# Sketch attention and squared-ReLU FFN: sketch features by TensorE products, block transposes and squares on VectorE, denominators as an extra column of kv

## The chip, the cores and the metric

One core of a Trainium2 chip. The time is device microseconds of one execution; medians of several executions are quoted. A profile's span is one or two microseconds shorter than the time of its run. The engines are TensorE (PE in the profile, PEld for its weight loads), VectorE (DVE), ScalarE (ACT), GpSimd (POOL) and SyncE (SP), which issues most DMAs. A run is called slow when it lies more than 1.5% above the fastest of its kernel.

## The reference, cut to what matters

```
q, k, v: (4 batches, 4 heads, 1088, 32);  S1, S2: (8, 32)      all fp32
phi(x)[i, j] = (S1 x)[i] * (S2 x)[j]            # 64 features of a token and head
kv  = sum over tokens of phi(k) v               # 64 x 32 per head
z   = sum over tokens of phi(k)                 # 64 per head
att = (phi(q) kv) / (phi(q) z + 1e-6)
x   = att as (4352 tokens, 128)
out = relu(x w_in)^2 w_out                      # 128 -> 2048 -> 128
```

## The kernel before: what the change and the argument touch

Tokens are handled in tiles of 128. The sketch products S1 x and S2 x are made by hand: GpSimd permutes q and k, GpSimd and VectorE multiply them with a broadcast row of S1 and S2 (4096 products per token for q and k together), VectorE adds in eights and GpSimd finishes the sums.

```python
for ti in range(2):                       # q, k
    for h in range(H):
        onpool = pcnt < NPOOL_PROD        # 3 of 8 on GpSimd
        pcnt += 1
        eng = nc.gpsimd if onpool else nc.vector
        src1 = ssperm if onpool else ssp_ps
        eng.tensor_tensor(                # L351
            out=_pap(Pa, 0, ns, 2048 * ti + 512 * h, [[1, 512]]),
            in0=_pap(xP, 0, ns, 128 * ti + 32 * h, [[0, 16], [1, 32]]),
            in1=_pap(src1, 0, ns, 0, [[32, 16], [1, 32]]), op=mult)
nc.vector.tensor_reduce(                  # L357
    out=Vt[0:ns, :], in_=_pap(Pa, 0, ns, 0, [[8, 512], [1, 8]]), axis=AX, op=add)
# ... GpSimd: Vt -> Wt -> av (two halvings), then 64 feature products per head
# ... TensorE transposes the features of q and k tile by tile into qkT; ScalarE copies
```

The denominators have a path of their own in each batch's "tail": z by a VectorE sum, broadcast by TensorE, permuted copies and products on GpSimd (`qpP`, `Pd`), and three more VectorE sums (`Vd`, `Wd`, `den`). The FFN runs in chunks of 512, 512 and 64 tokens:

```python
nc.tensor.matmul(pg[:, 0:nt], w_in[:, 128*c : 128*c+128], xT[:, t0 : t0+nt])   # fp16
nc.scalar.activation(gt[:, 0:nt], pg[:, 0:nt], Relu)
nc.scalar.activation(g2[:, 0:nt], gt[:, 0:nt], Square)
nc.tensor.matmul(po[:, 0:nt], w_o[:, 128*c : 128*c+128], g2[:, 0:nt], ...)      # fp32
```

## Time and profile before

| | |
|---|---|
| time, median of 4 runs | 553.76 us (550.21 to 558.77) |
| first FFN product starts | 187.9 us |
| last VectorE-heavy stretch ends | about 490 us |

Page of the kernel before: busy time per engine, then the span in 40 equal slices, where a digit is the busy share in tenths (PEclk: the granted TensorE clock in tenths).

```profile
PE 360.0 (66%) x1562; PEld 217.6 (40%) x1562; DVE 400.7 (73%) x652; ACT 225.6 (41%) x562; POOL 322.5 (59%) x726
...
PE   1021222591445599997455999984439999999996
...
DVE  1899996799999996889999968789997120580000
...
POOL 0999997579954685589846865897553000530000
PEclk9999999999999999995555999955559998559998
```

VectorE stands mostly at 8 or 9 in the first three quarters; TensorE is nearly idle in the first third and busy after. No average tells this: the windows view of the kernel before does, with the busy time of each engine in three stretches (then clock, DMA share, GB/s).

```profile
20.00:183.00 163.00, 57.34 (x276) 42.51 (x276) 153.53 (x189) 18.02 (x35) 135.40 (x302) 1.00 0.14 22
183.00:440.00 257.00, 201.82 (x879) 116.26 (x880) 220.71 (x348) 138.27 (x342) 167.41 (x371) 0.79 0.08 16
440.00:549.00 109.00, 98.78 (x406) 58.30 (x404) 20.97 (x108) 66.08 (x184) 12.35 (x33) 0.82 0.03 9
```

The columns after the length are PE, PEld, DVE, ACT, POOL. The clock of 1.00 in the first line is no measurement: this trace has no clock record before 192.7 us, and the views count such time as full clock. The durations say otherwise (18 instructions of `kv_ps` took 2.20 us at 111.7 us and 1.28 at 225.7). For 163 us VectorE is 94% busy and TensorE 35%; only the last 109 us belong to TensorE. The groups view of the kernel before (line, engine, operation, tiles, count; busy us and mean ns of one; idle before it):

```profile
L357 DVE TENSOR_REDUCE Vt<-Pa 128x512 f32<-128x4096 f32 (+1 forms) x36 | 158.6, 4406 | 0.2
L351 POOL TENSOR_TENSOR Pa<-xP,ssperm 128x512 f32<-128x512 f32 (+1 forms) x108 | 134.7, 1258 | 0.0
L351 DVE TENSOR_TENSOR Pa<-xP,ssp_ps 128x512 f32<-128x512 f32 (+1 forms) x180 | 114.9, 672 | 5.9 <-POOL xP L336 5.9
```

The sketch products and their first sum are 273.5 us of VectorE's 400.7. The chain of waits of the kernel before, by engine:

```profile
PE 40%; DVE 28%; POOL 20%; issue 7%; ACT 5%; DMA 0%; ACTq 0%; SPq 0%; POOLq 0%
```

### The profile page before, as it was taken

To read this page: it belongs to the slowest core of one execution; us is meant where nothing else is said; L and a number is where in the kernel's file an instruction comes from. 1 tells how busy PE (TensorE), PEld (TensorE's weight loads), DVE (VectorE), ACT (ScalarE), POOL (GpSimd) and SP (SyncE) were. 2 spreads that over 40 slices of the span, in tenths; PEclk is the share of its full clock that TensorE was granted. 3 is DMA by queue.
4 is the path that set the end of the run, shared out by engine and by line. 5 is a ranking of instruction groups with operands and counts; after the bars stand their busy time and mean duration, and the time that the engine had idled before them with its cause. 6 is when DMAs were issued, how large, how long until landed. Compare 5 with 4: busy or idle time off the path is not lost.

```text
span 549.1 us, 5863 instructions
## 1 busy us (share of the span) xinstructions
PE 360.0 (66%) x1562; PEld 217.6 (40%) x1562; DVE 400.7 (73%) x652; ACT 225.6 (41%) x562; POOL 322.5 (59%) x726
## 2 busy tenths in 40 slices
PE   1021222591445599997455999984439999999996
PEld 0011111470334244466342444673313346973334
DVE  1899996799999996889999968789997120580000
ACT  2010111011000389672003896720018977118885
POOL 0999997579954685589846865897553000530000
PEclk9999999999999999995555999955559998559998
DMA  5431011012000001022000010000000000000000
GB/s 163 69 61 19 14 20 20 11 24 36 7 10 10 10 11 38 11 38 39 10 10 12 11 39 11 20 16 1 0 2 2 10 11 19 4 0 1 11 9 22
DMA packets 61424, 11.39 MB, mean 21 GB/s; under 512 B 54864, under 2 KB 61264, under 8 KB 61264
## 3 DMA queue, kind: packets, MB, share of 16 engines
q1 hardware_dynamic: 61392, 11.02, 10.4%
q8 instruction: 12, 0.20, 0.1%
q14 instruction: 20, 0.16, 0.1%
HBM read 8.78 MB, written 2.23 MB: 20 GB/s over the span
## 4 chain that ended last, share of the span: by engine, by line
PE 40%; DVE 28%; POOL 20%; issue 7%; ACT 5%; DMA 0%; ACTq 0%; SPq 0%; POOLq 0%
PE po L114 24%; POOL Pa L351 9%; DVE Vt L357 9%; PE pg L105 5%; DVE Pa L351 4%; PE kv_ps L189 3%; DVE Wd L231 3%; DVE xs_big L271 3%; POOL xP L336 3%; DVE den L243 2%; POOL qpP L207 2%; POOL qp_big L387 2%; POOL Wt L370 2%; ACT gt L112 1%; DVE Vd L225 1%
## 5 line engine op out<-in xcount | busy, mean ns | idle before, releaser
L357 DVE TENSOR_REDUCE Vt<-Pa 128x512 f32<-128x4096 f32 (+1 forms) x36 | 158.6, 4406 | 0.2
L351 POOL TENSOR_TENSOR Pa<-xP,ssperm 128x512 f32<-128x512 f32 (+1 forms) x108 | 134.7, 1258 | 0.0
L351 DVE TENSOR_TENSOR Pa<-xP,ssp_ps 128x512 f32<-128x512 f32 (+1 forms) x180 | 114.9, 672 | 5.9 <-POOL xP L336 5.9
L112 ACT ACTIVATE gt<-pg 128x512 f32<-128x512 f32 (+1 forms) x192 | 82.1, 472 | 15.3 <-PE pg L105 15.0
L370 POOL TENSOR_TENSOR Wt<-Vt 128x256 f32<-128x256 f32 (+1 forms) x36 | 21.9, 609 | 72.1 <-DVE Vt L357 45.1
L213 POOL TENSOR_TENSOR Pd<-qpP,Zp_sb 128x256 f32<-128x256 f32 (+1 forms) x36 | 25.8, 727 | 52.5 <-ACT Zp_sb L199 52.5
L105 PE MATMUL pg<-xT,w_in 128*128 128x512 f16 (+1 forms) x192 | 53.1, 334 | 3.2 <-ACT gt L112 2.0
L336 POOL COPY xP<-qt 128x32 f32<-128x32 f32 (+1 forms) x144 | 27.6, 232 | 36.7 <-DVE Pa L351 23.8
L207 POOL COPY qpP<-qp_big 128x64 f32<-128x64 f32 (+1 forms) x144 | 37.9, 309 | 0.4
L177 DVE COPY zr<-zr_ps 1x64 f32<-1x64 f32 x16 | 3.3, 208 | 41.2 <-PE zr_ps L175 41.2
L105 PEld LDWEIGHTS <-w_in 128*128 128x128 f16 x192 | 20.1, 111 | 28.9 <-issue 26.9
L189 PE MATMUL kv_ps<-vt_big,kp_big 128*64 128x32 f32 (+1 forms) x288 | 27.9, 252 | 0.3 <-DVE zr L177 0.3
L336 POOL COPY xP<-kt 128x32 f32<-128x32 f32 (+1 forms) x144 | 27.7, 233 | 0.0
L189 PEld LDWEIGHTS kv_ps<-vt_big,kp_big 128*64 128x64 f32 (+1 forms) x288 | 24.7, 168 | 4.6 <-issue 1.1
L271 DVE TENSOR_SCALAR xs_big<-xs_big,rm 128x128 f32<-128x128 f32 (+1 forms) x36 | 23.7, 660 | 0.0
L231 DVE TENSOR_TENSOR Wd<-Vd 128x8 f32<-128x8 f32 (+1 forms) x36 | 23.7, 670 | 0.0
L387 POOL TENSOR_TENSOR qp_big<-av 128x256 f32<-128x256 f32 (+1 forms) x36 | 22.4, 621 | 0.2
L387 POOL TENSOR_TENSOR kp_big<-av 128x256 f32<-128x256 f32 (+1 forms) x36 | 22.4, 621 | 0.0
L243 DVE TENSOR_SCALAR den<-den 128x4 f32<-128x4 f32 (+1 forms) x36 | 20.7, 576 | 0.0
L196 ACT COPY kv_sb<-kv_ps 64x32 f32<-64x32 f32 x16 | 2.9, 180 | 37.4 <-PE kv_ps L189 37.3
L225 DVE TENSOR_REDUCE Vd<-Pd 128x16 f32<-128x256 f32 (+1 forms) x36 | 14.6, 405 | 3.5 <-POOL Pd L213 3.5
L290 ACT CAST xT<-xt_ps 128x128 f16<-128x128 f32 (+1 forms) x36 | 8.2, 258 | 19.0 <-PE xt_ps L285 19.0
(942 smaller groups left out, 780.9 us busy)
## 6 DMA issues: line engine op xcount, KB each, us to landing
qt<-in_q_dram SPq DMA_DIRECT2D x32, 64.0 KB, 2.0
kt<-in_k_dram SPq DMA_DIRECT2D x32, 64.0 KB, 2.2
vt_big<-in_v_dram SPq DMA_DIRECT2D x32, 64.0 KB, 2.4
out_dram<-ot_sb SPq DMA_DIRECT2D x32, 64.0 KB, 1.6
w_in_95<-in_moe_w_in_dram SPq DMA_DIRECT2D x1, 1024.0 KB, 5.1
w_o<-in_moe_w_out_dram SPq DMA_DIRECT2D x16, 64.0 KB, 2.0
vt_big<-in_v_dram SPq DMA_DIRECT2D x4, 32.0 KB, 2.2
qt<-in_q_dram SPq DMA_DIRECT2D x4, 32.0 KB, 2.1
```

Of the source, the lines that this page charges most:

```text
L105: nc.tensor.matmul(pg[:, 0:nt], w_in[:, 128 * c : 128 * c + 128], xT[:, t0 : t0 + nt],)
L112: nc.scalar.activation(gt[:, 0:nt], pg[:, 0:nt], Relu)
L114: nc.tensor.matmul(po[:, 0:nt], w_o[:, 128 * c : 128 * c + 128], g2[:, 0:nt], start=(g == 0 and cc == 0), stop=(g == 7 and cc == 1),)
L189: nc.tensor.matmul(kv_ps[:, :], _pap(kp_big, 0, ns, st * 256 + 64 * h, [[1, 64]]), _pap(vt_big, 0, ns, st * 128 + 32 * h, [[1, 32]]), star ...
L207: nc.gpsimd.tensor_copy(out=_pap(qpP, 0, ns, 64 * h, [[16, 4], [4, 4], [1, 4]]), in_=_pap(qp_big, 0, ns, st * 256 + 64 * h + 12, [[1, 4], ...
L231: nc.vector.tensor_tensor(out=Wd[0:ns, :], in0=_pap(Vd, 0, ns, 0, [[2, 8]]), in1=_pap(Vd, 0, ns, 1, [[2, 8]]), op=add,)
L271: nc.vector.tensor_scalar(out=_pap(xs_big, 0, ns, st * 128, [[1, 128]]), in0=_pap(xs_big, 0, ns, st * 128, [[1, 128]]), scalar1=rm[0:ns, 0 ...
L336: nc.gpsimd.tensor_copy(out=_pap(xP, 0, ns, 128 * ti + 32 * h, [[8, 4], [4, 2], [1, 4]]), in_=_pap(xt, 0, ns, 32 * h + 12, [[1, 4], [16, 2 ...
L351: eng.tensor_tensor(out=_pap(Pa, 0, ns, 2048 * ti + 512 * h, [[1, 512]]), in0=_pap(xP, 0, ns, 128 * ti + 32 * h, [[0, 16], [1, 32]]), in1= ...
L357: nc.vector.tensor_reduce(out=Vt[0:ns, :], in_=_pap(Pa, 0, ns, 0, [[8, 512], [1, 8]]), axis=AX, op=add,)
L370: nc.gpsimd.tensor_tensor(out=Wt[0:ns, :], in0=_pap(Vt, 0, ns, 0, [[2, 256]]), in1=_pap(Vt, 0, ns, 1, [[2, 256]]), op=add,)
L387: nc.gpsimd.tensor_tensor(out=_pap(pp_big, 0, ns, st * 256, [[64, 4], [8, 8], [1, 8]]), in0=_pap(av, 0, ns, 64 * ti, [[16, 4], [1, 8], [0, ...
```

## The change

Its intent: let TensorE do the sketch products, so that VectorE and GpSimd no longer bound the first part. Three named parts: features by fp32 products on TensorE (q and k transposed in 32x32 blocks by VectorE); the denominators as a 33rd column of kv (a column of ones beside v); squares on VectorE. With them comes a new structure: whole-batch loads of q and k; q features made already transposed, so no features are transposed afterwards; FFN chunks of 384, 384 and 320 tokens; and the attention of batch b+1 spread over the FFN of batch b, one piece for each four FFN steps. Cut to its core:

```diff
-  # permuted copies, products Pa, sums Vt, Wt, av; feature products on GpSimd; transposes
+  nc.vector.transpose(kT[:, c0:c1], kn[:, c0:c1])          # 32x32 blocks; L159, q: L162
+  nc.tensor.matmul(kf[0:w, ...64], kT[:, 128*t : 128*t+w], sk[:, :])        # L170, fp32
+  nc.scalar.copy(fb, second half of kf)
+  nc.vector.tensor_tensor(out=kp, in0=kf broadcast, in1=fb broadcast, op=mult)   # L187
+  nc.tensor.matmul(kvp[:, 66*pr : 66*pr+66], kp 128 columns, va 66 columns, ...) # L197
+  # q: features of two heads at a time, 64 rows of S1 / S2 and of q
+  nc.tensor.matmul(pa[:, 0:n], sqa[64*pr : 64*pr+64, :], qT[64*pr : 64*pr+64, c0:c0+n])  # L217
+  nc.scalar.copy(sa[:, 0:n], pa[:, 0:n])
+  nc.tensor.matmul(pb[:, 0:n], sqb[64*pr : 64*pr+64, :], qT[64*pr : 64*pr+64, c0:c0+n])  # L224
+  nc.vector.tensor_tensor(out=qp[...], in0=pb[:, 0:n], in1=sa[:, 0:n], op=mult)           # L227
-  # z, zp, qpP, Pd, Vd, Wd
+  # column 32 of each head's 33 columns of nd is the denominator
+  nc.tensor.matmul(nd[0:w, o : o+66], qp[... w columns], kv_sb[:, 66*pr : 66*pr+66])      # L241
-  nc.scalar.activation(g2[:, 0:nt], gt[:, 0:nt], Square)
+  nc.vector.tensor_tensor(out=g2[:, 0:n], in0=gt[:, 0:n], in1=gt[:, 0:n], op=mult)        # L321
+  for t0, t1 in CHUNKS:
+      for i, _ in enumerate(ffn_gen(b, t0, t1)):
+          if i % 4 == 2:
+              next(nxt, None)                  # a piece of attn_gen(b + 1)
```

## The prediction

> **What bounds the kernel now.** Page part 1: VectorE 400.7 us busy of 549 (73%), TensorE 360.0, GpSimd 322.5, ScalarE 225.6. Windows view: from 20 to 200 us almost only attention runs (VectorE 82 and 89 us of each 90, TensorE 24 and 49); from 200 to 440 attention of the next batch and FFN overlap, VectorE 85% busy; after 440 FFN remains, bound by TensorE and ScalarE. The chain of waits is PE 40%, DVE 28%, POOL 20%. Sketch features are made by hand (groups view): products (POOL 134.7, DVE 114.9 us) and an eight-wide sum (DVE 158.6 us). The squares cost ScalarE 0.63 us per 512 columns.
>
> **What the change does (estimates, per batch).**
> - TensorE. FFN stays: per 512 columns the trace has 0.213 us for the fp16 product and 0.86 for the fp32 one at full clock, so 0.8 us for 384; 36 us per batch. Added: 45 fp32 products with new 128-column weights and 64 or 66 moving columns. Four such of 32 columns (nd) took 1.08 us at full clock and 1.91 at half, so about 0.30 each: 14 us; four streams of 1088 columns: 7 us; transposes 2. About 59 us, 236 in all.
> - VectorE. Loses products, sums and the denominator's small ops. Gets squares, 48 x 0.48 us = 23; tails 8; feature products 6; block transposes 2.5. The Trainium skill, "VectorE: DVE Perf Modes", section "Mode 1× (REGULAR) — the baseline", gives one result per cycle; the trace agrees (512 elements in 0.672 us). About 40, 160 in all.
> - ScalarE. Relu 48 x 0.47 = 23 us, plus copies: 33; about 135 in all.
> - GpSimd: from 322 to a few us.
> - DMA: whole-batch q and k loads, 16 v loads of 128-byte rows. About 0.5 us of issue each, hidden.
>
> So the bound moves from VectorE plus GpSimd to TensorE, and FFN of batch b runs beside attention of b+1 throughout. The program order puts several first-layer products ahead of the second-layer ones, so I expect few stalls.
>
> **Time.** Opening: loads, transposes, attention of batch 0 with a cold TensorE, first FFN product at about 34 us (before: about 183). Then FFN 145 + attention of three batches 69 + rest of batch 0 6 = 220 us, with 8% for waits: 238. Output tail 4, clock dips 9: **285 us**, range 262 to 325. Chances: faster by over 2% 0.99, within 2% 0.005, slower 0.005.
>
> The clock matters: in the second half of the trace the same work ran at 0.5 whenever TensorE was sparse or fed by short products (250-300, 357-410, 462-492 us). The Trainium skill, "TensorE: Matmul & The Clock Gate", Part 1, says the array runs at half rate when idle; 1.08 against 1.91 us agrees. The denser stream should hold full clock nearly throughout after the opening.
>
> **What would show it right.** TensorE busy over 85% from 40 us on; granted clock near 1.0; VectorE near 160 us, ScalarE near 135, GpSimd under 15; the chain of waits dominated by PE (po, pg); squares about 0.5 us; first FFN product near 34 us.
>
> **What would make it wrong.** (a) Each FFN step now crosses ScalarE and VectorE, in-order queues: a square behind a block of tail ops, or a wait for the single-buffered attention accumulator in TensorE's order, would stall TensorE; then TensorE idles on DVE, and 320 us. (b) Bursts of short fp32 products drop the clock to 0.5 in each batch: 5 to 15 us more per batch. (c) Block transposes or PSUM-read feature products much slower than one element per cycle. (d) A longer opening, if loads come late.

## The result and the profile after

The changed kernel takes 288.06 us (287.52 to 288.63, 4 runs), against 553.76 us. The ratio is 0.5207, 95% interval 0.5188 to 0.5227. Here and below a ratio is the mean time of one kernel's fast runs over that of the other's of the same rounds, so not quite the ratio of the quoted medians. The prediction was 285 us, range 262 to 325.

Page of the kernel after, the same rows as before:

```profile
PE 260.4 (91%) x1104; PEld 157.9 (55%) x1104; DVE 153.9 (54%) x441; ACT 114.2 (40%) x302; POOL 2.2 (1%) x17
...
PE   0578996999999999999989999999899999999991
...
DVE  0810106569634587937346788655345784653550
...
POOL 2000000000000000000000000000000000000000
PEclk9999999999999999999999999999999999999997
```

TensorE is busy from slice 7 to the end, VectorE about half the time, GpSimd not at all. Chain of waits of the kernel after, by engine and by line:

```profile
PE 86%; DVE 4%; ACT 3%; DMA 3%; issue 2%; ACTq 0%; DVEq 0%
PE po L322 43%; PE pg L315 10%; PE pb L224 7%; PE kvp L197 7%; PE nd L241 7%; PE pa L217 6%; PE kf L170 4%; ACT gt L320 2%; DMA kn<-in_k_dram 2%; PE op L337 2%; DVE qp L227 1%; PE xp L300 1%; ACT oT L331 0%; ACT sa L222 0%; DMA s_nat<-in_S_dram 0%
```

Windows view of the kernel after, the columns as before, from the first FFN product on:

```profile
53.30:60.00 6.70, 6.70 (x21) 4.11 (x22) 4.82 (x17) 2.79 (x8) 0.00 (x0) 1.00 0.00 0
60.00:280.28 220.28, 215.29 (x965) 128.37 (x963) 133.63 (x379) 102.02 (x274) 0.16 (x1) 1.00 0.08 21
```

From 60 us to the last FFN product TensorE is 98% busy. So the story of the prediction holds, and the total too. But its first stage does not: the first FFN product came at 53.3 us, not at 34. The timeline of the kernel after shows why. Twelve instructions of `nd`, the second group of batch 0 and then the same group of batch 1:

```profile
50.73 2.77 PE L241 MATMUL nd<-kv,qp 128*128 128x66 f32 x12
...
106.76 1.50 PE L241 MATMUL nd<-kv,qp 128*128 128x66 f32 x12
```

Until about 58 us TensorE runs at half rate, although it is 76 to 100% busy in each 10 us from 10 us on. Note that the PEclk row says 9 up to the last slice. The row counts time before the first clock record as full clock, and the first record of this trace starts at 58.4 us, with full clock; so the row does not show a cold start, and the durations do. The Trainium skill, "TensorE: Matmul & The Clock Gate", section "Seeing it yourself", warns that the recorded clock events can be unreliable; here the record at 58.4 us agrees with the durations, and only the row read from the records is wrong, by a factor of two for the 48 us before it.

So three questions are left. Why was the opening cold for so long? If the opening took 19 us more than predicted, what took 19 us less? And which parts of the change brought the 266 us?

### The profile page after: what moved, and what is told of

The parts are those of the page before. It is cut to its first block, busy times and chain, and to the rows that moved or that the text cites. A ratio compares the mean times of both kernels' runs of the same rounds, so it can differ in the third digit from the quotient of the medians.

```text
span 286.6 us, 3493 instructions
## 1 busy us (share of the span) xinstructions
PE 260.4 (91%) x1104; PEld 157.9 (55%) x1104; DVE 153.9 (54%) x441; ACT 114.2 (40%) x302; POOL 2.2 (1%) x17
## 4 chain that ended last, share of the span: by engine, by line
PE 86%; DVE 4%; ACT 3%; DMA 3%; issue 2%; ACTq 0%; DVEq 0%
PE po L322 43%; PE pg L315 10%; PE pb L224 7%; PE kvp L197 7%; PE nd L241 7%; PE pa L217 6%; PE kf L170 4%; ACT gt L320 2%; DMA kn<-in_k_dram 2%; PE op L337 2%; DVE qp L227 1%; PE xp L300 1%; ACT oT L331 0%; ACT sa L222 0%; DMA s_nat<-in_S_dram 0%
## 5 line engine op out<-in xcount | busy, mean ns | idle before, releaser
L320 ACT ACTIVATE gt<-pg 128x384 f32<-128x384 f32 (+1 forms) x192 | 78.2, 480 | 70.3 <-PE pg L315 68.2
L315 PE MATMUL pg<-xTb,w_in 128*128 128x384 f16 (+1 forms) x192 | 47.4, 323 | 2.6 <-ACT gt L320 2.1
L224 PE MATMUL pb<-qT,sqb 64*128 64x512 f32 (+1 forms) x48 | 25.2, 610 | 3.7 <-DVE qp L227 2.0
L217 PE MATMUL pa<-qT,sqa 64*128 64x512 f32 (+1 forms) x48 | 25.7, 621 | 0.9 <-DVE qp L227 0.9
L197 PEld LDWEIGHTS kvp<-va,kp 128*128 128x128 f32 (+1 forms) x144 | 22.0, 225 | 6.3 <-issue 5.5
L170 PE MATMUL kf<-sk,kT 128*128 128x64 f32 (+1 forms) x72 | 13.8, 334 | 12.4 <-DVE sk L125 10.3
L197 PE MATMUL kvp<-va,kp 128*128 128x66 f32 (+1 forms) x144 | 23.1, 309 | 0.0
L241 PE MATMUL nd<-kv,qp 128*128 128x66 f32 (+1 forms) x144 | 22.1, 294 | 0.0
L241 PEld LDWEIGHTS nd<-kv,qp 128*128 128x128 f32 (+1 forms) x144 | 20.2, 208 | 2.8 <-issue 1.5
L187 DVE TENSOR_TENSOR kp<-kf,fb 128x256 f32<-128x256 f32 (+1 forms) x36 | 13.2, 411 | 6.4 <-PE kvp L197 5.1
```

The lines of the kernel that those rows point to most:

```text
L170: nc.tensor.matmul(kf[0:w, 64 * i : 64 * i + 64], kT[:, 128 * (t0 + i) : 128 * (t0 + i) + w], sk[:, :],)
L187: nc.vector.tensor_tensor(out=_ap(kp, 0, w, 256 * i, [[64, 4], [8, 8], [1, 8]]), in0=_ap(kf, 0, w, 64 * i, [[16, 4], [1, 8], [0, 8]]), in1 ...
L197: nc.tensor.matmul(kvp[:, 66 * pr : 66 * pr + 66], _ap(kp, 0, w, 256 * i + 128 * pr, [[1, 128]]), _ap(va, 0, w, t * H * 33 + 66 * pr, [[1, ...
L217: nc.tensor.matmul(pa[:, 0:n], sqa[64 * pr : 64 * pr + 64, :], qT[64 * pr : 64 * pr + 64, c0 : c0 + n])
L224: nc.tensor.matmul(pb[:, 0:n], sqb[64 * pr : 64 * pr + 64, :], qT[64 * pr : 64 * pr + 64, c0 : c0 + n])
L241: nc.tensor.matmul(nd[0:w, o : o + 66], qp[:, pr * S + 128 * t : pr * S + 128 * t + w], kv_sb[:, 66 * pr : 66 * pr + 66],)
```

## The experiments

Twelve kernels ran, in three groups; each group shares its own runs of the kernel before (medians 553.3, 553.5 and 554.0 us). All gave correct results except one that is wrong.

### 1. Query-feature weights padded to 128 rows

The changed kernel; the weights of S1 and S2 for a pair of heads get 64 rows of zeros, so that the product uses all 128 rows for the same columns.

```diff
-  sqa = cpool.tile([128, 128], F32)            # sqb alike
+  sqa = cpool.tile([128, 256], F32)
-  c = 64 * (h % 2)
+  c = 64 * h
-  pa[:, 0:n], sqa[64*pr : 64*pr+64, :], qT[64*pr : 64*pr+64, c0 : c0+n]
+  pa[:, 0:n], sqa[:, 128*pr : 128*pr+128], qT[:, c0 : c0+n]      # pb alike
```

> The changed kernel with the query-feature weights padded by zeros from 64 to 128 rows: the same columns streamed, the same number of products, only twice the rows of the array in use. Question: why the opening lasts 53 us and TensorE runs at half rate in it although it is 83 to 100% busy. Theory R (the clock control weighs the part of the array in use, so 64-row streams count as half idle): the clock rises by about 20 us, the eight 512-column query products take half their time, the first FFN product comes near 40 us instead of 53, and the time falls from 288 to 272-279. Rival G (the waits between products in the opening keep the clock low, whatever the rows): durations in the opening stay, time 286-290.

Measured: 280.22 us (278.78 to 280.48), ratio to before 0.5066 (the changed kernel: 0.5207). Faster by 8 us than the changed kernel, in neither range: just above theory R's and well below rival G's. The first FFN product starts at 51.4 us, and the clock did not rise by 20 us. It rose at 41.4, by the trace's first clock record. Timeline of TensorE at that point, first in the kernel after, then in this one:

```profile
36.85 1.22 PE L217 MATMUL pa<-qT,sqa 64*128 64x512 f32 x1
37.11 0.85 PE L197 MATMUL kvp<-va,kp 64*128 64x66 f32 x3
37.87 1.05 PE L217 MATMUL pa<-qT,sqa 64*128 64x512 f32 x1
38.72 1.91 PE L224 MATMUL pb<-qT,sqb 64*128 64x512 f32 x2
...
43.31 0.69 PE L217 MATMUL pa<-qT,sqa 64*128 64x64 f32 x2
```

```profile
36.90 2.08 PE L217 MATMUL pa<-qT,sqa 128*128 128x512 f32 x2
38.77 1.91 PE L224 MATMUL pb<-qT,sqb 128*128 128x512 f32 x2
...
42.21 0.39 PE L217 MATMUL pa<-qT,sqa 128*128 128x64 f32 x2
```

Both kernels stream nearly the same columns (the kernel after has three short `kvp` instructions more), almost without a gap, from 36.9 to 40.5 us. After it the 128-row kernel is at full rate (a 64-column pair takes 0.39 us) and the 64-row kernel is not (0.69 us; its first clock record starts at 58.4 us). So the rows in use matter. They do not suffice: from 14.6 to 26 us the padded kernel streamed about 2.07 us of each 2.8 with 128 rows and stayed cold. Nor do 128 rows without a gap, if the products are short. Timeline of the padded kernel, at half rate (0.21 us from one start to the next):

```profile
27.71 5.65 PE L197 MATMUL kvp<-va,kp 128*128 128x66 f32 x26
```

By 45.9 us, after a wait and short products, it was cold again (recorded fall at 44.8 us).

Of the 8 us, only 1.9 came before the first FFN product. The others came later, at full clock, and have another cause. Timeline of TensorE, in the kernel after and then in this one:

```profile
81.27 0.81 PE L322 MATMUL po<-g_602,w_o 128*128 128x384 f32 x2
...
83.14 1.02 PE L224 MATMUL pb<-qT,sqb 64*128 64x512 f32 x2
84.08 0.91 PE L322 MATMUL po<-g_609,w_o 128*128 128x384 f32 x2
84.93 1.12 PE L217 MATMUL pa<-qT,sqa 64*128 64x512 f32 x2
```

```profile
80.33 1.02 PE L224 MATMUL pb<-qT,sqb 128*128 128x512 f32 x2
81.18 0.81 PE L322 MATMUL po<-g,w_o 128*128 128x384 f32 x2
81.83 1.02 PE L217 MATMUL pa<-qT,sqa 128*128 128x512 f32 x2
```

From the start of `pb` to the start of `po` are 0.94 us after and 0.85 here; from `po` to `pa` 0.85 and 0.65. A change between 64-row and 128-row products costs 0.1 to 0.2 us. The trace of the kernel after holds 64 such changes from 60 us on, so 6 to 13 us in all (an estimate), against the 6 us to be explained. The Trainium skill, "TensorEngine Tiling (Array Packing)", section "Key Properties", says that changing the tiling mode drains TensorE; these steps agree. It also says that tiles work in parallel, and the kernel after did that now and then, when `pb` of one pair of heads and `pa` of the other, on the two halves of the rows, stood side by side:

```profile
90.78 0.69 PE L224 MATMUL pb<-qT,sqb 64*128 64x512 f32 x1
90.78 0.69 PE L217 MATMUL pa<-qT,sqa 64*128 64x512 f32 x1
```

Padding gives that up, and was faster all the same.

### 2. TensorE warmed up while the loads run

The changed kernel; 30 dummy fp16 products of 512 columns, of a tile set to 1.0, are issued first.

```diff
+  wz = cpool.tile([128, 512], F16)
+  nc.vector.memset(wz[:], 1.0)
+  wps = psf.tile([128, 512], F32, tag="po", bufs=1)
+  for _ in range(30):
+      nc.tensor.matmul(wps[:, :], wz[:, 0:128], wz[:, :])
```

> The changed kernel with 30 dummy fp16 products of 512 columns issued while the first loads are under way (about 1 to 11 us), so that TensorE enters the opening at full clock; the rest is untouched. Theory R (64-row streams count as half idle): the key features from 10 to 13 us run at full rate, then the clock falls back within some us of the 64-row streams; gain 2 to 5 us, time 283-286. Rival G (only the start was cold; once warm, 85% busy keeps it warm): the opening stays warm, first FFN product near 38 us, time 270-276. A third outcome, no gain at all, would say that the dummy work delays the opening as much as it helps.

Measured: 285.49 us (284.78 to 286.2), ratio 0.5166: 2.6 us less than the changed kernel, in theory R's range; rival G is out. Here the warm start gives a clock record before the opening: it falls at 14.3 us and rises again at 55.3. Timeline of TensorE in this kernel:

```profile
10.30 1.52 PE L175 MATMUL kf<-sk,kT 128*128 128x64 f32 x12 [0.91 <-DVE sk L130]
...
14.00 1.72 PE L222 MATMUL pa<-qT,sqa 64*128 64x512 f32 x2
16.49 2.04 PE L229 MATMUL pb<-qT,sqb 64*128 64x512 f32 x2 [0.77 <-ACT sa L227]
```

The key features took 1.52 us (2.79 in the kernel after); the second 64-row product is back at 2.04. The fall comes 0.3 us after the start of the first 64-row product, behind short products and a wait of 1.2 us, so this fall alone does not speak against 64 rows; that the clock stayed low for 41 us does.

### 3. Both together

The edits of 1 and 2.

> Both of the above together. Theory R: full clock from 10 us to the end; first FFN product near 36 us, time 266-274. Rival G: no better than the warm-up alone.

Measured: 269.84 us (268.08 to 271.41), ratio 0.4893, within theory R's range. Timeline of TensorE, the same two products as in 2, now with 128 rows:

```profile
13.96 1.10 PE L222 MATMUL pa<-qT,sqa 128*128 128x512 f32 x2
15.82 1.10 PE L229 MATMUL pb<-qT,sqb 128*128 128x512 f32 x2 [0.77 <-ACT sa L227]
```

At full rate, with the same gaps as in 2; the first FFN product starts at 37.6 us. The two edits bring 18 us together, and 8 and 3 alone. In the opening of run 1 it took long 128-row products back to back to get warm. For staying warm one profile is not enough: run 12 has the same opening with 128 rows, and there the clock fell at 16.0 us, but was back at 22.8. The clocks of all executions tell more. The mean granted clock was 0.921 to 0.927 in the four of run 2 and 0.958 to 0.979 in the four here, which is 41 to 45 us at half rate against 11 to 23 (an estimate: twice the missing share, times the span). So rows count in keeping the clock too. Half of the rows hold zeros, so it is not the useful arithmetic that counts. Rows are not all of it here either: by 35 us, after a wait and short products, the clock was low again (twelve instructions of `nd` in 2.77 us), and full by about 45 us, within the first block of FFN products.

### 4. Attention of batches 1 to 3 left out

The changed kernel; wrong (relative error 1.0): every batch's FFN reads the x of batch 0.

```diff
-      issue_loads(b + 1)
-      nxt = attn_gen(b + 1)
+      xT[b + 1], betas[b + 1] = xT[0], betas[0]
```

> The changed kernel with the attention of batches 1 to 3 left out: the FFN of every batch reads the x of batch 0. The result is wrong on purpose. Theory (TensorE-bound, as predicted: the attention of a batch costs its own 23 us of TensorE time beside the FFN of the batch before): the time falls by about 69 us, to 216-224. Rival (FFN steps leave waits on ScalarE and VectorE which attention products fill): the time falls by under 55 us, to 233 or more, and TensorE shows idle time on VectorE in the FFN stretch.

Measured: 238.34 us (237.58 to 238.94). Three batches of attention cost 288.06 - 238.34 = 49.7 us, not 69: the rival's range. TensorE's busy time fell by 260.4 - 205.6 = 54.8 us, or 18.3 per batch where the prediction had 23. So the larger part of the miss is that attention takes less of TensorE's time than costed (two instructions of `nd`, which make one product, take 1.50 / 6 = 0.25 us at full clock, predicted 0.30), and about 5 us of it take no time of their own. The FFN's waits are there. Timeline of this kernel, one round of five FFN steps:

```profile
135.77 0.62 PE L315 MATMUL pg<-xTb,w_in 128*128 128x320 f16 x2 [0.25 <-ACT gt L320]
...
136.29 2.45 PEld L322 LDWEIGHTS po<-g,w_o 128*128 128x128 f32 x10 [0.43 <-DVE g L321]
136.30 2.96 PE L322 MATMUL po<-g,w_o 128*128 128x320 f32 x10
```

TensorE waits for Relu and then for the first square of the next five; full rounds of 320 columns all take 4.12 to 4.15 us. From one such group of `po` to the next are 136.30 - 132.17 = 4.13 us, where the stream alone needs 5 x (0.133 + 0.5375) = 3.35 us (0.213 and 0.86 us per 512 columns of the prediction, times 320/512). That is 19% of the round lost, yet the profile has TensorE 95% busy from 100 to 220 us: part of what it calls busy is the start and end of each group. The Trainium skill, "Trainium Kernel Development and Optimization", section "Performance Expectations", calls TensorE's busy time a bad measure of distance from the limit because products are pipelined; this run agrees.

### 5. The features alone, on the kernel before

The kernel before; per tile, TensorE transposes q and k and multiplies with block-diagonal S1 and S2. The products `Pa` and sums `Vt`, `Wt` go. Everything else stays, GpSimd's feature products too.

```diff
+  for ti, xt in enumerate((qt, kt)):
+      nc.tensor.transpose(kf[:, 128*ti : 128*ti+ns], xt[0:ns, :], iden[0:ns, 0:ns])
+  nc.vector.tensor_copy(xTt, kf)
+  for ti in range(2):
+      nc.tensor.matmul(kf[0:ns, 256+64*ti : 320+64*ti], xTt[:, 128*ti : 128*ti+ns], sk[:, :])
+  nc.vector.tensor_copy(av[0:ns, :], kf[0:ns, 256:384])
```

> The kernel before with one part of the change alone: the sketch features by TensorE (a 128x128 transpose and one fp32 product against block-diagonal S1 and S2 per tile of q and of k) in place of the products and sums on VectorE and GpSimd; loads, feature products, denominators, FFN as before. Theory V (hand-made features on VectorE and GpSimd bound the kernel before): VectorE busy falls from 400 to about 150 us, GpSimd from 322 to about 140, and the time from 554 to 350-400 us, with the rest bound by TensorE at partly half clock. Rival (TensorE, already 40% of the chain of waits, takes over at once): time stays above 450.

Measured: 437.64 us (434.3 to 443.3), ratio 0.7891. A gain of 116 us, in neither range. VectorE fell to 131.4 us and GpSimd to 104.9, somewhat below the 150 and 140 expected, but TensorE took over at 389.4 us busy, 88% of the span, and much of it at half clock. Windows view of this kernel (its profile is of the slowest run, 443.3 us, so only the shape is read from it; runs 9 and 10 show the same):

```profile
40.00:60.00 20.00, 16.29 (x91) 12.57 (x92) 8.12 (x15) 1.69 (x5) 3.62 (x6) 0.50 0.19 30
...
220.00:240.00 20.00, 19.82 (x89) 9.19 (x87) 6.15 (x7) 14.66 (x31) 1.21 (x2) 1.00 0.07 18
```

Where attention stands alone, the clock (third figure from the right) is 0.50 with TensorE 81% busy; where FFN streams, 1.00.

### 6. The denominators alone, on the kernel before

```diff
-  vt_big ... NST * 128;   kv_ps 64x32;   z4, zr, zrp, zp_ps, qpP, Pd, Vd, Wd
+  vt_big ... NST * 132, every 33rd column 1.0;   kv_ps 64x33;   nd4 128x4x33
+  nc.vector.tensor_scalar(out=den, in0=_pap(nd4, 0, ns, 32, [[33, 4]]), scalar1=1e-6, ..., op0=add)
```

> The kernel before with the second part alone: denominators as a 33rd column of kv (a column of ones beside v), in place of z sums, the permuted copies and products on GpSimd and the tree of sums on VectorE. VectorE loses about 75 us of busy time, GpSimd about 65. Theory V (VectorE sets the pace in the first 440 us): time 480-510. Rival (the GpSimd chain of feature work sets the pace): above 535.

Measured: 483.57 us (480.57 to 484.18), ratio 0.873: 70 us less, in theory V's range. VectorE's busy time fell from 400.7 to 311.0 us, by more than the 75 expected, and GpSimd's from 322.5 to 261.6. The rival's range is missed. But the edit takes work off both engines, so it does not show that VectorE alone set the pace. In the chain of waits GpSimd even falls by more, from 20% of 549 us to 6% of 479 (110 to 29 us), and VectorE from 28% to 23% (154 to 110 us). What the run shows is that the two together set the pace.

### 7. The squares on VectorE alone, on the kernel before

```diff
-  nc.scalar.activation(g2[:, 0:nt], gt[:, 0:nt], Square)
+  nc.vector.tensor_tensor(out=g2[:, 0:nt], in0=gt[:, 0:nt], in1=gt[:, 0:nt], op=mult)
```

> The kernel before with the third part alone: the squares on VectorE in place of ScalarE. VectorE gets about 85 us more work. Theory V: this part only pays once VectorE is freed; alone it makes the kernel slower, 575-605 us. Rival (ScalarE was a bound of the FFN stretches, so its relief shows): 549 us or less.

Measured: 647.23 us (640.32 to 650.56), ratio 1.1658: 93 us slower, more than the range of theory V. In its profile (of the slowest run, 650.56 us) VectorE's busy time is 114 us higher, not 85. And a square now stands in an in-order queue behind sums of 4.4 us each. Longest waits that involve the squares, in the waits view of this kernel (waiter, what it waited for; total us, times, longest):

```profile
PEld po L116 <- DVE g L113: 122.5, 105, 11.8
...
ACT gt L112 <- DVE g L113: 98.1, 48, 10.8
```

TensorE waited 122.5 us for squares, up to 11.8 us at a time.

### 8. The squares back on ScalarE, in the changed kernel

```diff
-  nc.vector.tensor_tensor(out=g2[:, 0:n], in0=gt[:, 0:n], in1=gt[:, 0:n], op=mult)
+  nc.scalar.activation(g2[:, 0:n], gt[:, 0:n], Square)
```

> The changed kernel with the third part undone: squares back on ScalarE. ScalarE then has about 205 us of work, some 52 us of each batch's 57. Theory Q (an in-order ScalarE that close to full delays the steps that TensorE waits for): 300-320 us, with TensorE idle on ScalarE. Rival (only the total counts, TensorE still has more): within 2% of 288.

Measured: 289.54 us (289.51 to 290.26), ratio 0.5237: about 0.5% slower than the changed kernel, in the rival's range. Theory Q falls. ScalarE's busy time rose from 114.2 to 187.0 us, VectorE's fell from 153.9 to 67.0, and TensorE's is 262.6. The third named part brings about 1.5 us, compared over two groups of runs.

### 9 and 10. Two, then all three named parts, on the kernel before

The edits of 5 and 6; then those of 5, 6 and 7.

> The kernel before with two parts together: features by TensorE and denominators as a kv column. Alone they saved 116 and 70 us. If the savings add (both are VectorE work on the critical path): 368 us. Theory S (with the features gone VectorE is only 30% busy, so the denominators' VectorE work is hidden; what is left to save are their TensorE products at half clock and the serial stretch of the last batch): 400-428 us.

Measured: 397.10 us (395.63 to 398.04), ratio 0.7175. Together the two parts save 157 us, not 186, so the savings do not add; theory S is nearer, and its range is missed by 3 us.

> The kernel before with all three named parts (features, denominators, squares on VectorE) but its own loads, tile sizes, transposes of the features and order of FFN and attention. Theory T (the rest of the gain of the change comes from its new structure: feature products made already transposed, FFN of one batch beside attention of the next throughout, so that TensorE streams enough to keep its clock): about as fast as b_feat_den, within 4%, and far above 288. Rival (the three parts explain the gain): below 330 us.

Measured: 409.47 us (404.15 to 411.61), ratio 0.7373: theory T. With all three named parts the kernel before is still 121 us slower than the changed one, and the squares cost it 12 us even with VectorE freed. Windows view of run 10, an attention stretch and an FFN stretch:

```profile
240.00:260.00 20.00, 16.73 (x72) 12.98 (x73) 9.35 (x62) 5.44 (x14) 1.21 (x2) 0.50 0.01 3
...
100.00:120.00 20.00, 19.58 (x70) 8.23 (x67) 9.54 (x16) 11.43 (x23) 0.30 (x1) 1.00 0.08 17
```

Its TensorE has 363.2 us of busy time where the changed kernel has 260.4. Part of that is the half clock in the attention stretches and part the transposes of features (`tps`, 10% of the chain of waits in run 9 and in run 10), which the new structure does not have. How the 121 us divide was not measured. They also hold what run 5 did in its own way: its transposes of q and k are by TensorE, where the changed kernel has block transposes on VectorE.

### 11. The second FFN product in fp16

The changed kernel; one pass over the columns in place of four, as the durations have it (0.86 us per 512 columns in fp32, 0.213 in fp16). x is scaled to 32 in place of 1024 so that squares fit in fp16.

```diff
-  w_o = cpool.tile([128, DFF], F32);  g2 = fpool.tile([128, 384], F32, tag="g2")
+  w_o = cpool.tile([128, DFF], F16)   # copied from the fp32 load by ScalarE
+  g2 = fpool.tile([128, 384], F16, tag="g2")
-  scalar1=1.0 / 1024.0, scalar2=1.0 / 1024.0
+  scalar1=1.0 / 32.0, scalar2=1.0 / 32.0
```

> The changed kernel with the second FFN product in fp16 (one pass over the columns in place of four; squares written as fp16, x scaled to 32 in place of 1024 so that squares fit; checked against the reference). It takes 0.48 us per step, 92 us in all, off TensorE and leaves the other engines' work as it is. Theory (after the opening TensorE alone sets the pace): the time falls until VectorE's and ScalarE's 40 and 33 us per batch are met, to 205-240 us. Rival (waits across ScalarE and VectorE set the pace behind a busy-looking TensorE): above 265.

Measured: 228.84, 239.84, 240.33 and 248.32 us. Only the fastest counts as fast, so there is no ratio. The fast one and one slow one are in the theory's range, the other two above its end at 240, and all four lie well below the rival's 265. The squares kept their time (0.55 us for 384 columns in both kernels). So TensorE does set the pace after. The spread goes with the clock: the mean granted clock of the four is 0.945, 0.903, 0.902 and 0.859. Windows view of one of the slow ones:

```profile
80.00:90.00 10.00, 10.00 (x15) 2.22 (x15) 2.79 (x6) 2.92 (x6) 0.00 (x0) 0.50 0.47 135
90.00:100.00 10.00, 10.00 (x24) 4.29 (x23) 3.67 (x8) 3.00 (x8) 0.00 (x0) 0.50 0.00 0
...
180.00:190.00 10.00, 10.00 (x31) 3.35 (x30) 4.60 (x8) 4.31 (x10) 0.00 (x0) 1.00 0.07 20
```

The clock records have it at half clock from 68.8 to 109.7 us. TensorE was fully busy from 70 to 108 us, first with `kvp`, then mostly with the query features of 64 rows. That the long fp32 FFN products, now gone, would have kept the clock up is not tested apart. It is what (b) of the prediction feared for the changed kernel, where it did not come.

### 12. The version that the experiments point to

The edits of 1, 2 and 11, and Relu's output in fp16 as well.

> The changed kernel with padded feature weights, the warm-up products, the fp16 second product and fp16 Relu output (so that the square reads 16-bit operands): what the experiments so far point to. Expected: e_f16 less the 18 us that padding and warm-up brought together and less what the faster squares free: 180-212 us, correct.

Measured: 183.40, 183.43, 189.13 and 189.46 us, correct; the first two count as fast and give a ratio to before of 0.3317 (0.3292 to 0.3342). It beats both kernels; against the changed one the two ratios give 0.3317 / 0.5207 = 0.64. TensorE is 91% busy, VectorE 65%, ScalarE 62%. The squares of 16-bit operands took 339 ns on average. In the opening the clock fell here as well, with 128 rows, but it came back (recorded at 16.0 and 22.8 us):

```profile
15.78 1.86 PE L230 MATMUL pb<-qT,sqb 128*128 128x512 f32 x2 [0.77 <-ACT sa L228]
...
22.93 3.01 PE L203 MATMUL kvp<-va,kp 128*128 128x66 f32 x26
```

The first pair takes 1.86 us in place of 1.10; the 26 short products take 3.01 us where they took 5.65 at half rate in run 1. From 43.3 us to 179.8 the clock was full in this execution, past the attention in which run 11 lost it; the two slow executions lost more (0.922 in place of 0.957). Its second product is of lower precision than both kernels'; the first was fp16 in all of them.

## Why the prediction was right, point by point

The total was right: 285 predicted, 288.06 measured, 3 us apart, well inside 262 to 325. Two of its terms were wrong by 19 us each and cancelled; that the total came this close is luck.

| term | predicted us | measured us | read from |
|---|---|---|---|
| opening, to the first FFN product | 34 | 53.3 | timeline after |
| attention of batches 1 to 3 | 69 | 49.7 | run 4 |
| FFN, rest of batch 0, waits, clock dips | 145 + 6 + 18 + 9 = 178 | 226.98 - 49.7 = 177.3 | windows after, less run 4 |
| output tail | 4 | 286.6 - 280.28 = 6.3 | timeline after |

The measured lines sum to the span, 286.6 us, by the way they were made.

- **"The bound moves from VectorE plus GpSimd to TensorE": right.** The chain of waits is 86% PE; TensorE is 98% busy from 60 us; taking passes off TensorE (run 11) takes time off the kernel, and taking the squares off VectorE (run 8) does not. Before, run 6 takes 90 us off VectorE and 61 off GpSimd and gains 70 us.
- **"First FFN product at about 34 us": wrong, the term that failed.** Of its kind, (d) of the prediction feared late loads. They do not explain it: k was there at 6.6 us, the first key-feature product ran at 10.3, and no later wait of TensorE in the opening is put down to a load. The 43 us from there to the first FFN product went to TensorE's own work at half rate, with products of 2.07 us between waits. The prediction did say "with a cold TensorE", but 34 us leaves only 24 after 10.3, about its own 23 us for one batch's attention at full clock; at half rate the same figure gives 10.3 + 2 x 23 = 56 us (an estimate), near the 53.3 measured. The cold start was named and, it seems, not charged. Runs 1 to 3 show the clock as the cause: with a warm start and 128-row products the same work ends at 37.6 us, which is 15.7 of the 19 us.
- **"The denser stream should hold full clock nearly throughout after the opening": right.** The records have full clock from 58.4 to 283.7 us, and from 60 us on the short products (`kf`, `kvp`, `nd`) follow each other by at most 0.16 us, where half rate gave 0.21. The 9 us set aside for dips were not needed. But the reason given, density, was only half of it: in the opening a stream 76 to 100% busy stayed at half rate for 48 us. What the FFN brings is long products on all 128 rows; that these hold the clock up is inferred from run 1, not tested in the FFN itself.
- **"45 products of about 0.30 each: 14 us": too dear.** At full clock 0.25. TensorE's busy time for a batch of attention is 18.3 us (run 4), predicted 23, and 16.6 of it is time.
- **"8% for waits": too low for the FFN alone, right in sum.** Run 4 shows 19% of an FFN round lost to the way over ScalarE and VectorE; with attention beside it some of the gaps are filled. With the dips that did not come, the third line of the table fits by luck as much as by sense.
- **Engine totals.** VectorE 153.9 us (predicted 160), GpSimd 2.2 (under 15), ScalarE 114.2 (135; too high, partly since Relus of 0.45 to 0.50 us overlap their neighbours and sum to 78 us, not 90). Squares took 0.48 us for 320 columns and 0.55 for 384. Feature products from PSUM (0.41 us for 256 elements) and block transposes (0.69 to 0.75 us for 512 and 576 columns) were no trouble, so (c) did not come true. Feature products of q took 211 ns for 64 columns and 691 for 512, so 1.07 ns a column and about 0.14 us fixed (an estimate from these two). That fits the one-result-per-cycle rule cited in the prediction, whose single figure, 512 elements in 0.672 us, holds the fixed part too.
- **What the prediction did not ask: which part pays.** Features alone 116 us, denominators alone 70, both 157; the squares cost 93 us alone and bring 1.5 in the changed kernel; the remaining 121 us (409 to 288) come with the structure, not with the three named parts.

What stays open: the exact rule of the clock. The runs show that rows, the length of products and gaps all count, but none finds how many rows or how long a stream it takes, and executions of one kernel differ (0.958 to 0.979 in run 3).

## What to carry to other kernels

When attention-like work goes from VectorE to TensorE, cost it at both clock rates and ask which products bring the clock up: in the opening here 64-row products and short products with new weights did not, long 128-row ones did, and padding the rows with zeros made the kernel faster. Judge a moved piece of work by the engine that sets the pace at that point: the same move of the squares cost 17% in one kernel and nothing in the other. And when a total comes out right, check its stages all the same: here two errors of 19 us hid each other.

## What the Trainium skill lacked or had wrong

- "TensorE: Matmul & The Clock Gate", Part 1, says that about 3.4 us of sustained activity warm the array. It does not say that the rows in use count. In run 1 long 128-row fp32 products from 36.9 us on had the clock up at 41.4 us; nearly the same columns on 64 rows in the same time did not. Nor does it say that the length of products counts: 26 short instructions on 128 rows, 5.65 us without a gap, stayed at half rate.
- The same page, "HAM oscillation", lays the fall of the clock to idle gaps. It does not cover a clock that stays down under load: in run 11 it fell at 68.8 us, with no wait of TensorE over 1.04 us in the 15 us before, and stayed at 0.50 to 109.7 us with TensorE fully busy.
- The same page warns of unreliable clock records. It could add a plain case: there is no record before the first change (58.4 us in the changed kernel, 192.7 in the kernel before), so a view that counts this time as full clock misses durations that are nearly doubled (nd x12: 2.77 against 1.50 us).
- "TensorEngine Tiling (Array Packing)", "Key Properties", names the drain at a change of tiling mode without a figure. Here a change between 64-row and 128-row products cost 0.1 to 0.2 us (0.94 against 0.85, and 0.85 against 0.65 us).
